# Loading the first pair's values before the third pair's queries and keys, and moving the third pair's roundings and first scores behind head 0's products

## The chip, the cores and the metric

One core of a Trainium2 chip runs the whole program. The metric is the device time of one execution in microseconds; a run is one execution, and the time given for a kernel is the median of its runs. The engines that the text names are TensorE (PE, with its weight loads PEld), VectorE (DVE), ScalarE (ACT), GpSimd (POOL) and SyncE (SP), which issues the DMAs.

## The reference

Attention with a decay, over 8 batches of 8 heads (576 positions, 64 columns each), and then a soft mixture of 8 small experts on the 4608 resulting rows. The change lies in the attention alone.

```python
scores = scale * np.matmul(q, k.transpose(0, 1, 3, 2))
log_f = np.log(np.clip(f, 0.0001, 1.0))
cum = np.cumsum(log_f, axis=-1)
decay = cum[:, :, :, None] - cum[:, :, None, :]
scores = np.where(causal, -1000000000.0, scores + decay)
scores = scores - np.max(scores, axis=-1, keepdims=True)
attn = np.exp(scores)
attn = attn / (np.sum(attn, axis=-1, keepdims=True) + 1e-09)
return np.matmul(attn, v).astype(np.float32)
...
logits = x @ phi
...
slot_input = d.T @ x
...
    h = np.maximum(slot_input[e] @ w1[e], 0.0)
    slot_out[e] = h @ w2[e]
...
return (c @ slot_out).astype(np.float32)
```

## The kernel before

The 64 heads are taken as 32 pairs (index g), two heads to a pair (h, or i = 2g + h over all heads). The program is written out in the order in which each engine runs it: an engine starts its instructions strictly in that order, each as soon as the counts that it waits for are reached.

A head goes through these steps. `load_qk` (L174) and `load_v` (L178) bring a pair's queries and keys (tile RAW, 576 KB) and its values (tile V, 325 KB) from memory. `round_k` and `round_q` (L183, L188, ACT) round keys and queries into WA and YA; `low_k` and `low_q` (L209, L214, POOL) compute what the rounding left off, into WB and YB, which also get a copy of the rounded part by DMA (`dup_k` L199, `dup_q` L203). `load_cum` (L194) brings the decay sums into two rows of WA. `s1` (L230, PE) makes a first set of scores in four pieces, each in a bank `s` of which there are three, and `tops` (L244, L246, DVE) takes their row maxima into MT. `mturn` (L256, PE) turns the maxima into a row, in columns 384 to 511 of the bank `pv` of that head; `mrows` copies that row out (L265, ACT, into the tile `mr`, of which there is one) and sends it by DMA into a row of YA (L268). `s2` (L283, L284, PE, banks `ring`) makes the exact transposed scores with the maxima taken off, `expo` (L290, ACT) their exponentials in PTS, `causal` (L298, L301, POOL) zeroes what lies above the diagonal. `s3` (L315, PE) multiplies them with the values into columns 0 to 324 of `pv`, one bank for each head of a pair; one entry of its list is one product of 64 queries with one block of keys, and the trace shows two matmul records for it. `norm` (L330 to L335, DVE) divides, and `px` (L342, PE) turns the result.

Heads 0 to 3 and the first pieces of head 4 are written out by hand, where the change lies; from g = 1 on a loop runs, one pass for a pair, in which the scores of heads 2g + 3 and 2g + 4 are made between those of heads 2g and 2g + 1. Its first instruction on PE is `s2` of head 2 (tile YA with 67 rows). `first(i, n)` is piece n of `s1` and its `tops`; `both(i, n)` is a piece of `s2` and its `expo`. The lists of `s3`, for head h:

```python
SIDES = [[x for n in zip(units(h, 0, range(4)), units(h, 1, range(4))) for x in n] for h in range(2)]
LAST = [units(h, h, (4,)) for h in range(2)]
```

`SIDES[h]` has 20 entries and `LAST[h]` 5. DMAs are all issued by SP, in program order, and spread over the core's DMA engines.

Of the kernel before, what the change touches and what calls it, by code (L numbers as in the profile page):

```python
# [47 lines left out]
def pt_col(c, i):  # L48
    at = {}
    for bank, cc, i0, w in SEGS:  # L50
        o = at.get(bank, 0)
        at[bank] = o + w
        if cc == c and i0 <= i < i0 + w:
            return SEG_O[bank] + o + i - i0
    raise ValueError


def queries(t, u):

    if t == 4:  # L60
        return 8
    return 2 * u + t if t < 2 else 4 + 2 * (1 - u) + t - 2


def units(h, u, ts):

    return [(h, t, u, c) for t in ts for c in range(queries(t, u) // 2 + 1)]


SIDES = [[x for n in zip(units(h, 0, range(4)), units(h, 1, range(4))) for x in n] for h in range(2)]  # L70
LAST = [units(h, h, (4,)) for h in range(2)]
# [3 lines left out]
def attn_softmoe(ctx: ExitStack, tc: tile.TileContext, qk, v, f, phi, w1, w2, cst, out):  # L75
# [78 lines left out]
    def pair(g):  # L154
        return 0 <= g < NG
# [15 lines left out]
    def load_qk(g):  # L171
        if pair(g) and ("r", g) not in st:
            st["r", g] = RAW[g % 3]
            nc.sync.dma_start(RAW[g % 3], qk[g])  # L174

    def load_v(g):
        if pair(g):
            nc.sync.dma_start(V[:, g % 2], v[g])  # L178

    def round_k(g, *hs):  # L180
        if pair(g):
            for h in hs or range(2):
                nc.scalar.copy(WA[g % 3][0:64, S * h : S * h + S], RAW[g % 3][64:128, h])  # L183

    def round_q(g, *hs):
        if pair(g):
            for h in hs or range(2):
                nc.scalar.copy(YA[g % 3][0:64, h, 64:640], RAW[g % 3][0:64, h])  # L188

    def load_cum(g):  # L190
        if pair(g):
            r0, r1 = CUM[g % 3]
            dst = WA[g % 3][r0 : r1 + 1 : r1 - r0, 0 : 2 * S].rearrange("c (h s) -> c h s", h=2)
            nc.sync.dma_start(dst.bitcast(F32), cumd[:, g].rearrange("h c s -> c h s"))  # L194

    def dup_k(g, h0=0, h1=2):
        if pair(g):
            s = slice(S * h0, S * h1)
            nc.sync.dma_start(WB[g % 2][64:128, s].bitcast(F32), WA[g % 3][0:64, s].bitcast(F32))  # L199
# [11 lines left out]
    def low_q(i):  # L211
        if head(i):
            g, h = divmod(i, 2)
            nc.gpsimd.tensor_tensor(YB[g % 2][64:128, h], RAW[g % 3][0:64, h], YA[g % 3][0:64, h, 64:640].bitcast(F32), op=ALU.subtract)  # L214
# [4 lines left out]
    def s1(i, *which):  # L219

        if not head(i):
            return
        g, h = divmod(i, 2)
        ya, wa, m = YA[g % 3], WA[g % 3][:, S * h : S * h + S], TOP[g % 3]
        for n in which:
            bank, o, blk, j0, w = TOPS[n]
            if o == 0:
                st["top", i % 2, bank] = scratch(False, f"s{i}_{bank}")
            t = st["top", i % 2, bank]
            nc.tensor.matmul(  # L230
                t[:, o : o + w], ya[0:m, h, 128 * blk : 128 * blk + 128], wa[0:m, j0 : j0 + w], start=True, stop=True
            )

    def tops(i, *which):
        if not head(i):
            return
        g, h = divmod(i, 2)
        for n in which:
            bank, o, blk, j0, w = TOPS[n]
            t = st["top", i % 2, bank]  # L240
            m0 = max(448 - (128 * blk + 64) + j0, 0)
            top = MT[g % 3][:, NBLK * h + blk : NBLK * h + blk + 1] if g else m2[h][:, blk, 1:2]
            if n == 2:
                nc.vector.tensor_reduce(top, t[:, o : o + w], axis=AX.X, op=ALU.max)  # L244
                continue
            nc.vector.tensor_tensor_reduce(  # L246
                out=t[:, o : o + w], in0=t[:, o : o + w], in1=mask[:, m0 : m0 + w], scale=1.0, scalar=top.bitcast(F32) if n == 3 else -3.0e38,
                op0=ALU.add, op1=ALU.max, accum_out=top,
            )

    def mturn(g, h0=0, h1=2):

        if not pair(g):
            return
        pm = pv[h0 and 1][:, 384:512]
        nc.tensor.transpose(pm[0 : NBLK * (h1 - h0), 0:128].bitcast(F32R), MT[g % 3][:, NBLK * h0 : NBLK * h1], turner)  # L256
        st["pm", g, h0] = pm

    def mrows(g, h0=0, h1=2):

        if not pair(g):
            return
        n = NBLK * (h1 - h0)
        mr = small.tile([2 * NBLK, P], F32R, name=f"mr{g}_{h0}", tag="mr", bufs=1)
        nc.scalar.copy(mr[0:n], st["pm", g, h0][0:n, 0:128])  # L265
        m = TOP[g % 3]
        dst = YA[g % 3][m : m + 1, h0:h1].rearrange("c h s -> c (h s)")
        nc.sync.dma_start(dst.bitcast(F32), mr[0:n].bitcast(F32))  # L268

    def s2(i, *which):  # L270
        if not head(i):
            return
        g, h = divmod(i, 2)
        ya, wa, yb, wb, m = YA[g % 3], WA[g % 3], YB[g % 2], WB[g % 2], TOP[g % 3] + 1
        for n in which:
            bank, c, i0, w = SEGS[n]
            t, at = (turn(), 0) if n < 4 else st["bank"]

            n = 128 if c < 4 else 64
            o = t[0:n, at : at + w]  # L280
            at += w
            j0 = S * h + 128 * c
            nc.tensor.matmul(o, wa[0:m, j0 : j0 + n], ya[0:m, h, 64 + i0 : 64 + i0 + w], start=True, stop=False)  # L283
            nc.tensor.matmul(o, wb[:, j0 : j0 + n], yb[:, h, i0 : i0 + w], start=False, stop=True)  # L284
            st["bank"] = t, at

    def expo(i, bank):
        if head(i):
            t, at = st["bank"]
            nc.scalar.activation(PT[i % 2][:, SEG_O[bank] : SEG_O[bank] + at], t[:, 0:at], AF.Exp, scale=0.125)  # L290

    def causal(i):

        if not head(i):
            return
        pt = PT[i % 2]
        d3 = pt[:, 0:960].rearrange("p (a b) -> p a b", b=320)[:, :, 0:128]
        nc.gpsimd.affine_select(d3, d3, pattern=[[0, 3], [1, 128]], compare_op=ALU.is_ge, fill=0.0, base=0, channel_multiplier=-1)  # L298
        for o, w in ((pt_col(3, 384), 128), (pt_col(4, 512), 64)):
            dd = pt[:, o : o + w]  # L300
            nc.gpsimd.affine_select(dd, dd, pattern=[[1, w]], compare_op=ALU.is_ge, fill=0.0, base=0, channel_multiplier=-1)  # L301
# [9 lines left out]
    def s3(g, todo):  # L311
        for h, t, u, c in todo:
            r = queries(t, u)
            at = pt_col(c, 64 * r)
            nc.tensor.matmul(  # L315
                pvv[h][64 * u : 64 * u + 64, t, :], PT[h][:, at : at + 64], V[:, g % 2, c, 65 * h : 65 * h + 65], start=(c == 0), stop=(c == r // 2)
            )
# [4 lines left out]
    def norm(i):  # L322
        if not head(i):
            return
        g, h = divmod(i, 2)
        b, p = divmod(g, NPAIR)
        x, o = xtile(b, p // 2), pvv[h]
        at = 128 * (p % 2) + 64 * h
        rl = small.tile([P, NBLK], F32, name=f"rl{i}", tag="rl")
        nc.vector.tensor_scalar_add(rl, o[:, :, 64], EPS)  # L330
        nc.vector.reciprocal(rl, rl)  # L331
        rl = rl.rearrange("p (t o) -> p t o", o=1)
        for ts in (slice(0, NBLK),) if i < NH - 1 else (slice(0, NBLK, 4), slice(1, 4)):
            to = x[:, ts, at : at + 64]
            nc.vector.tensor_tensor(to, o[:, ts, 0:64], rl[:, ts].broadcast_to(list(to.shape)), op=ALU.mult)  # L335
# [177 lines left out]
    def warm(n, a, w=192):  # L513

        for _ in range(n):
            nc.tensor.matmul(ring[0][:, 0:w], a[:, 0:128], a[:, 0:w], start=True, stop=True)  # L516
# [75 lines left out]
    round_k(1, 0)  # L592
    dup_k(1, 0, 1)
    load_cum(2)
    load_qk(2)
    load_v(0)

    def first_rows(h):
        part = ((0, 4), (4, 5))
# [12 lines left out]
    def first(i, n, busy=0):  # L612
        s1(i, *GROUPS[n])
        warm(busy, cs)
        tops(i, *GROUPS[n])

    def both(i, n):
        s2(i, *((0,), (1,), (2,), (3, 4, 5))[n])
        expo(i, n)
# [44 lines left out]
    both(1, 2)  # L664
    first(3, 2)
    first(3, 3)
    round_k(2, 0)
    round_q(2, 0)
    both(1, 3)
    causal(1)  # L670
    low_k(3)
    low_q(3)
    s3(0, SIDES[0][:20])
    first(4, 0)
    mturn(1, 1, 2)
    mrows(1, 1, 2)
    round_k(2, 1)
    round_q(2, 1)
    dup_q(2)
    dup_k(2)  # L680
    s3(0, SIDES[0][20:] + LAST[0])
    first(4, 1)
    first(4, 2)
    first(4, 3)
    norm(0)
    s3(0, LAST[1] + SIDES[1])
    load_cum(3)

    def fresh(stack, name, n):
# [469 lines left out]
```

## Time and profile before

| | |
|---|---|
| median of 3 runs | 385.81 us (385.1 to 386.08) |
| profiled execution | 385.02 us |
| its span | 383.3 us |
| PE, PEld busy | 95%, 86% |
| DVE, ACT, POOL busy | 74%, 70%, 67% |
| granted TensorE clock, mean | 0.986 |

The span is from the first to the last instruction that the profile records; the profiled execution's own time is 1.7 us more. Busy shares are averages over the whole span.

### The profile page before, as it was taken

What the parts mean: (1) busy time and instruction counts of PE and PEld (TensorE: products, weight loads), DVE (VectorE), ACT (ScalarE), POOL (GpSimd) and SP (SyncE); (2) the same over time, 40 slices, a digit from 0 to 9 for tenths busy, and PEclk for the clock granted to TensorE, in tenths of its full rate; (3) what the DMA queues carried; (4) which work ended last, traced back from release to release, by engine and by line L of the source; (5) the groups of instructions that cost most, each with busy time, mean ns of one, the idle gap of its engine ahead of it and who ended that gap; (6) DMA issues with size and microseconds to landing.
All of it is one profiled execution on the core that took longest, in us unless ns stands there. A gap on an engine that the chain in (4) does not pass through costs nothing.

```text
span 383.3 us, 15238 instructions
## 1 busy us (share of the span) xinstructions
PE 365.8 (95%) x5900; PEld 328.9 (86%) x5900; DVE 283.2 (74%) x1080; ACT 270.2 (70%) x656; POOL 258.6 (67%) x369
## 2 busy tenths in 40 slices
PE   8989999999999999999999999999999999999950
PEld 7888999999999999999999999999999986556650
DVE  7878887888878888888888888887888636443670
ACT  8859887878787878787878787878787654113550
POOL 4987887878797879787978797879787941010000
PEclk9999999999999999999999999999999999999995
DMA  6785778777868687768777777777777889999998
GB/s 190 197 207 163 227 232 264 203 224 210 252 180 249 195 251 197 231 197 245 208 216 218 225 215 220 213 221 216 218 214 213 264 290 377 414 405 393 310 326 291
DMA packets 37488, 93.72 MB, mean 245 GB/s; under 512 B 4412, under 2 KB 14380, under 8 KB 37416
## 3 DMA queue, kind: packets, MB, share of 16 engines
q1 hardware_dynamic: 37416, 92.75, 78.5%
q8 instruction: 46, 0.75, 0.8%
q14 instruction: 26, 0.21, 0.2%
HBM read 63.93 MB, written 9.73 MB: 192 GB/s over the span
## 4 chain that ended last, share of the span: by engine, by line
PE 91%; ACT 2%; DVE 1%; DMA 1%; POOL 1%; issue 0%; SPq 0%; DVEq 0%; POOLq 0%; ACTq 0%
PE pv L315 25%; PE ring L283 14%; PE s L230 13%; PE ring L284 13%; PE pv L342 4%; PE lg L389 3%; PE ring L516 2%; PE pv L1000 2%; PE ds L480 2%; PE ring L969 2%; PE pv L969 2%; PE ring L1000 2%; ACT PTS L290 1%; DMA V<-in_v 1%; PE ring L1084 1%; PE more L1084 1%
## 5 line engine op out<-in xcount | busy, mean ns | idle before, releaser
L290 ACT ACTIVATE PTS<-ring 128x320 f32<-128x320 f32 (+2 forms) x256 | 119.5, 500 | 38.1 <-PE ring L284 30.7
L283 PE MATMUL ring<-YA,WA 67*128 67x320 f32 (+9 forms) x384 | 118.8, 323 | 0.0
L246 DVE CUSTOM_DVE_ANT_0 s<-s,mask 128x320 f32<-128x320 f32 (+3 forms) x256 | 109.3, 445 | 8.1 <-PE s L230 2.4
L284 PE MATMUL ring<-YB,WB 128*128 128x320 f32 (+4 forms) x384 | 110.5, 296 | 0.0
L315 PE MATMUL pv<-V,PTS 128*64 128x65 f32 x3200 | 101.7, 223 | 1.1 <-POOL YB L214 1.0
L315 PEld LDWEIGHTS pv<-V,PTS 128*64 128x64 f32 x3200 | 96.9, 138 | 4.0 <-issue 1.2
L230 PE MATMUL s<-WA,YA 66*128 66x288 f32 (+9 forms) x384 | 97.9, 310 | 0.4 <-ACT PTS L290 0.3
L209 POOL TENSOR_TENSOR WB<-RAW,WB 64x576 fp32r<-64x576 f32 x64 | 90.9, 1420 | 10.5 <-DMA WB<-WA 5.4
L214 POOL TENSOR_TENSOR YB<-RAW,YA 64x576 fp32r<-64x576 f32 x64 | 89.8, 1421 | 2.5
L283 PEld LDWEIGHTS ring<-YA,WA 67*128 67x128 f32 (+3 forms) x384 | 68.9, 181 | 5.5 <-issue 2.1
L284 PEld LDWEIGHTS ring<-YB,WB 128*128 128x128 f32 (+1 forms) x384 | 69.9, 182 | 0.0
L230 PEld LDWEIGHTS s<-WA,YA 66*128 66x128 f32 (+1 forms) x384 | 63.0, 190 | 6.1 <-ACT YA L188 0.5
L246 DVE DVE_READ_ACCUMULATOR2_ANT MT<- 128x1 fp32r x310 | 43.9, 142 | 0.0
L301 POOL TENSOR_SCALAR_AFFINE_SELECT PTS<-PTS 128x128 f32<-128x128 f32 (+1 forms) x128 | 31.4, 266 | 17.1 <-ACT PTS L290 15.1
L183 ACT CAST WA<-RAW 64x576 fp32r<-64x576 f32 x63 | 39.5, 668 | 3.5 <-DMA RAW<-in_qk 2.7
L298 POOL TENSOR_SCALAR_AFFINE_SELECT PTS<-PTS 128x384 f32<-128x384 f32 x64 | 33.4, 522 | 12.7 <-ACT PTS L290 8.0
L188 ACT CAST YA<-RAW 64x576 fp32r<-64x576 f32 x62 | 39.4, 669 | 0.4
L246 DVE CUSTOM_DVE_ANT_0 s<-s,mask,MT 128x288 f32<-128x288 f32 x62 | 32.6, 526 | 9.0
L342 PE MATMUL pv<-cs,X 128*128 128x128 f32 x155 | 36.4, 272 | 0.0
L335 DVE TENSOR_TENSOR X<-pv,rl 128x320 f32<-128x320 f32 (+1 forms) x65 | 31.5, 486 | 2.4 <-DVE rl L331 0.3
L330 DVE TENSOR_SCALAR rl<-pv 128x5 f32<-128x5 f32 x64 | 10.5, 163 | 26.5 <-PE pv L315 21.1
L244 DVE TENSOR_REDUCE MT<-s 128x1 fp32r<-128x288 f32 x62 | 27.9, 451 | 0.7
(261 smaller groups left out, 383.5 us busy)
## 6 DMA issues: line engine op xcount, KB each, us to landing
w<-in_w SPq DMA_DIRECT2D x45, 512.0 KB
RAW<-in_qk SPq DMA_DIRECT2D x31, 576.0 KB
V<-in_v SPq DMA_DIRECT2D x32, 325.0 KB
YB<-YA SPq DMA_DIRECT2D x30, 288.0 KB
WB<-WA SPq DMA_DIRECT2D x30, 288.0 KB
p<-in_w SPq DMA_DIRECT2D x6, 512.0 KB
out<-RAW SPq DMA_DIRECT2D x12, 256.0 KB
out<-p SPq DMA_DIRECT2D x10, 256.0 KB
```

Source lines behind the costliest of these rows:

```text
L183: nc.scalar.copy(WA[g % 3][0:64, S * h : S * h + S], RAW[g % 3][64:128, h])
L188: nc.scalar.copy(YA[g % 3][0:64, h, 64:640], RAW[g % 3][0:64, h])
L209: nc.gpsimd.tensor_tensor(t[0:64], RAW[g % 3][64:128, h], t[64:128].bitcast(F32), op=ALU.subtract)
L214: nc.gpsimd.tensor_tensor(YB[g % 2][64:128, h], RAW[g % 3][0:64, h], YA[g % 3][0:64, h, 64:640].bitcast(F32), op=ALU.subtract)
L230: nc.tensor.matmul(t[:, o : o + w], ya[0:m, h, 128 * blk : 128 * blk + 128], wa[0:m, j0 : j0 + w], start=True, stop=True)
L246: nc.vector.tensor_tensor_reduce(out=t[:, o : o + w], in0=t[:, o : o + w], in1=mask[:, m0 : m0 + w], scale=1.0, scalar=top.bitcast(F32) if ...
L283: nc.tensor.matmul(o, wa[0:m, j0 : j0 + n], ya[0:m, h, 64 + i0 : 64 + i0 + w], start=True, stop=False)
L284: nc.tensor.matmul(o, wb[:, j0 : j0 + n], yb[:, h, i0 : i0 + w], start=False, stop=True)
L290: nc.scalar.activation(PT[i % 2][:, SEG_O[bank] : SEG_O[bank] + at], t[:, 0:at], AF.Exp, scale=0.125)
L298: nc.gpsimd.affine_select(d3, d3, pattern=[[0, 3], [1, 128]], compare_op=ALU.is_ge, fill=0.0, base=0, channel_multiplier=-1)
L315: nc.tensor.matmul(pvv[h][64 * u : 64 * u + 64, t, :], PT[h][:, at : at + 64], V[:, g % 2, c, 65 * h : 65 * h + 65], start=(c == 0), stop= ...
L342: nc.tensor.transpose(pm[:, 0:128], x[:, t, 128 * (p % 2) : 128 * (p % 2) + 128], ident)
```

## The change

In the part written by hand, four things move. Nothing is added or left out.

1. `load_v(0)` is issued before `load_qk(2)`.
2. The roundings of pair 2's first head (`round_k(2, 0)`, `round_q(2, 0)`) come after the last piece of head 1's scores and its exponential, not before.
3. All 25 products of head 0 come in one piece; `first(4, 0)`, which was between the 20th and the 21st, comes behind them.
4. `mturn(1, 1, 2)` and `mrows(1, 1, 2)` are now followed by eight products of head 1, and only then comes `first(4, 0)`, followed directly by the other three pieces of head 4's first scores.

```diff
     dup_k(1, 0, 1)
     load_cum(2)
+    load_v(0)
     load_qk(2)
-    load_v(0)
...
     first(3, 2)
     first(3, 3)
+    both(1, 3)
     round_k(2, 0)
     round_q(2, 0)
-    both(1, 3)
     causal(1)
     low_k(3)
     low_q(3)
-    s3(0, SIDES[0][:20])
-    first(4, 0)
+    s3(0, SIDES[0] + LAST[0])
     mturn(1, 1, 2)
     mrows(1, 1, 2)
+    s3(0, SIDES[1][:8])
+    first(4, 0)
     round_k(2, 1)
     round_q(2, 1)
     dup_q(2)
     dup_k(2)
-    s3(0, SIDES[0][20:] + LAST[0])
     first(4, 1)
     first(4, 2)
     first(4, 3)
     norm(0)
-    s3(0, LAST[1] + SIDES[1])
+    s3(0, LAST[1] + SIDES[1][8:])
     load_cum(3)
```

TensorE, from the first scores of head 4 on, before. In these rows pv_148 and pv_149 are the banks of head 0 and head 1, s_0 to s_3 the four pieces of head 4's first scores, WA_94 and YA_93 pair 2's rounded keys and queries, MT_109 the maxima of pair 1; a name in brackets is an engine, or a queue of DMAs, for whose count the row waits.

```order
L230 MATMUL s_0_395<-WA_94,YA_93 128x320 [waits DMAHW2_49,DMAHW7_49,DVE_49,Activation_49]
L230 MATMUL s_0_395<-WA_94,YA_93 128x192
L256 MATMUL pv_149<-turner,MT_109 5x128 [waits DVE_49]
L315 MATMUL pv_148<-V,PTS 64x65 x4
L315 MATMUL pv_148<-V,PTS 64x65 [waits Pool_49]
L230 MATMUL s_1_413<-WA_94,YA_93 128x288
L230 MATMUL s_2_416<-WA_94,YA_93 128x288
L230 MATMUL s_3_419<-WA_94,YA_93 128x448 [waits DVE_49]
L230 MATMUL s_3_419<-WA_94,YA_93 128x64
L315 MATMUL pv_149<-V,PTS 64x65 [waits Activation_49]
```

TensorE at the same place, with the change, from the last product of head 0 on.

```order
L315 MATMUL pv_148<-V,PTS 64x65 [waits Pool_49]
L256 MATMUL pv_149<-turner,MT_109 5x128 [waits DVE_49]
L315 MATMUL pv_149<-V,PTS 64x65 [waits Activation_49,Pool_49]
L315 MATMUL pv_149<-V,PTS 64x65 x7
L230 MATMUL s_0_412<-WA_94,YA_93 128x320 [waits DMAHW7_49,DMAHW2_49]
L230 MATMUL s_0_412<-WA_94,YA_93 128x192
L230 MATMUL s_1_421<-WA_94,YA_93 128x288
L230 MATMUL s_2_424<-WA_94,YA_93 128x288
L230 MATMUL s_3_427<-WA_94,YA_93 128x448 [waits DVE_49]
L230 MATMUL s_3_427<-WA_94,YA_93 128x64
L315 MATMUL pv_149<-V,PTS 64x65 x4
```

The first piece of head 4's scores has moved from before the turning to behind eight products of head 1, the wait for ACT has moved from that piece to the first of those products, and the four pieces now stand in a row.

ScalarE at that place; rows with a minus are those of before, mr_0 and mr_1 the copies of the maxima of pair 1's two heads (the second of them reads head 1's bank).

```order
 L265 CAST mr_0_340<-pv_148 5x128
 L290 ACTIVATE PTS<-ring_151 128x320
+L290 ACTIVATE PTS<-ring_152 128x512
 L183 CAST WA_94<-RAW_97 64x576
 L188 CAST YA_93<-RAW_97 64x576
-L290 ACTIVATE PTS<-ring_152 128x512
 L265 CAST mr_1_401<-pv_149 5x128
 L183 CAST WA_94<-RAW_97 64x576
```

The last exponential of head 1 has moved ahead of the two roundings of pair 2's first head; the copy of the second maxima stays behind both.

SyncE's DMAs at the place of the two loads.

```order
 L199 DMA WB_88<-WA_86 64x576
 L194 DMA WA_94<-cumd 2x2x576
-L174 DMA RAW_97<-in_qk 128x1152
-L178 DMA V<-in_v 128x650
+L178 DMA V<-in_v 128x650
+L174 DMA RAW_97<-in_qk 128x1152
 L203 DMA YB_87<-YA_85 64x576 x2
 L199 DMA WB_88<-WA_86 64x576
```

The two loads have changed places, and every other DMA stands where it stood.

## Rows read from the trace of the kernel before

**Rows 1.** The page: busy time, share of the span, instructions.

```profile
PE 365.8 (95%) x5900; PEld 328.9 (86%) x5900; DVE 283.2 (74%) x1080; ACT 270.2 (70%) x656; POOL 258.6 (67%) x369
```

**Rows 2.** Chain of waits, first 30 us: waiter, releaser, us, times, longest.

```profile
ACT mr L265 <- DMA YA<-mr: 2.1, 1, 2.1
```

**Rows 3.** Timeline, TensorE, 19.6 to 26.6 us: start, us, instructions [idle before].

```profile
19.60 0.22 PE L284 MATMUL ring<-YB,WB 128*64 128x64 f32 x1
20.83 1.39 PE L315 MATMUL pv<-V,PTS 128*64 128x65 f32 x40 [1.01 <-POOL YB L214]
22.15 0.50 PE L230 MATMUL s<-WA,YA 66*128 66x320 f32 x2
22.49 0.22 PE L256 MATMUL pv<-turner,MT 128*5 128x128 f32 x1
22.64 0.80 PE L315 MATMUL pv<-V,PTS 128*64 128x65 f32 x10
23.76 0.51 PE L230 MATMUL s<-WA,YA 66*128 66x448 f32 x2
24.20 1.96 PE L315 MATMUL pv<-V,PTS 128*64 128x65 f32 x50
26.09 0.47 PE L283 MATMUL ring<-YA,WA 67*128 67x448 f32 x1
```

**Rows 4.** Timeline, GpSimd: end of head 0's masking, and what follows.

```profile
18.78 0.49 POOL L301 TENSOR_SCALAR_AFFINE_SELECT PTS<-PTS 128x128 f32<-128x128 f32 x2
19.36 1.40 POOL L214 TENSOR_TENSOR YB<-RAW,YA 64x576 fp32r<-64x576 f32 x1
```

**Rows 5.** Timeline, ScalarE: rounding, last exponential of head 1, copy of the maxima.

```profile
19.09 0.67 ACT L183 CAST WA<-RAW 64x576 fp32r<-64x576 f32 x1
20.36 0.59 ACT L290 ACTIVATE PTS<-ring 128x512 f32<-128x512 f32 x1
23.06 0.26 ACT L265 CAST mr<-pv 5x128 fp32r<-5x128 f32 x1 [2.12 <-DMA YA<-mr]
```

**Rows 6.** Timeline, SyncE's issues: start and duration of the issue.

```profile
14.96 0.38 SPq L174 DMA_DIRECT2D RAW<-in_qk  x1
15.45 0.37 SPq L178 DMA_DIRECT2D V<-in_v  x1
18.44 0.76 SPq L268 DMA_DIRECT2D YA<-mr  x1
26.13 0.84 SPq L194 DMA_DIRECT2D WA<-cumd  x1
```

**Rows 7.** Busy time by windows: PE, PEld, DVE, ACT, POOL, clock, DMA share, GB/s.

```profile
16.00:18.00 2.00, 1.88 (x12) 1.49 (x11) 1.78 (x7) 1.34 (x3) 1.92 (x6) 1.00 0.93 286
24.00:26.00 2.00, 2.00 (x52) 1.86 (x51) 1.78 (x9) 0.68 (x2) 1.94 (x3) 1.00 0.11 23
...
53.00:61.70 8.70, 8.70 (x148) 8.37 (x146) 7.03 (x28) 7.22 (x18) 7.48 (x10) 1.00 0.87 250
```

**Rows 8.** Timeline, VectorE: maxima of head 4, then head 5's first and last.

```profile
22.69 0.50 DVE L246 CUSTOM_DVE_ANT_0 s<-s,mask 128x320 f32<-128x320 f32 x1 [2.09 <-PE s L230]
23.57 0.14 DVE L246 DVE_READ_ACCUMULATOR2_ANT MT<- 128x1 fp32r x1
23.81 0.46 DVE L244 TENSOR_REDUCE MT<-s 128x1 fp32r<-128x288 f32 x1
27.41 0.45 DVE L244 TENSOR_REDUCE MT<-s 128x1 fp32r<-128x288 f32 x1
30.26 0.14 DVE L246 DVE_READ_ACCUMULATOR2_ANT MT<- 128x1 fp32r x1
```

**Rows 9.** Timeline, TensorE weight loads around 30 us.

```profile
28.84 0.68 PEld L342 LDWEIGHTS pv<-cs,X 128*128 128x128 f32 x5
29.98 0.19 PEld L230 LDWEIGHTS s<-WA,YA 97*128 97x128 f32 x1 [0.47 <-ACT YA L188]
30.80 0.09 PEld L256 LDWEIGHTS pv<-turner,MT 128*10 128x10 f32 x1
```

## The prediction

> **What bounds the kernel now.** The page comes first: TensorE (PE) is busy for 365.8 us, 95% of the span [rows 1]. A stall of PE is time lost and a stall removed is time gained, unless a later stall swallows the difference. So the second view is the chain of waits over the first 30 us, where the change lies. It names one that comes to matter: ScalarE's copy of the maxima waited 2.1 us for the DMA that sends the earlier copy away [rows 2]. The third view is the timeline, engine by engine.
>
> PE ends head 1's scores at 19.60 + 0.22 = 19.82 and starts the first products at 20.83, after 1.01 us of standing [rows 3]. GpSimd's low part of pair 1's queries, named as releaser, ends just then, at 19.36 + 1.40 = 20.76 [rows 4]. But the products do not read it. What they need of GpSimd is head 0's masking, and that ended at 18.78 + 0.49 = 19.27 [rows 4]. The third thing they need is the values, whose load was issued at 15.45, behind the queries and keys of 14.96 [rows 6]. The DMA engines were 93% busy from 16 to 18 us, and down to 11% only from 24 on [rows 7]. I take it that the values landed near 20.8. The view prints no landing, so this is an inference; the other reading is a rival below.
>
> **The change, part by part.** The base is the profiled execution, 385.02 us (a span of 383.3 and 1.7 around it). The same difference is put on the median, 385.81. A measurement of this kernel can tell about 0.3% from no change, 1.16 us.
>
> *The two loads.* They keep their issue slots and their bytes, so what stands behind both should not move. The values come in front and queries and keys land where the values landed, near 20.8, 1.7 us later than the 19.09 at which ScalarE rounded them [rows 5]. PE can then start head 0's products at about 19.86 and not 20.83. Taken alone that is a gain of 1.0 us, its upper bound.
>
> *The roundings.* ScalarE first does head 1's last exponential (0.59 us, from about 19.85), then two roundings of 0.67 each [rows 5] from 20.8, done by 22.15. The copy behind them started at 23.06 [rows 5], so they fit with 0.9 us over. Cost nothing, as long as the load lands before 21.7.
>
> *Head 0's products.* In before 40 records took 22.15 - 20.83 = 1.32 us (33 ns each) and the last ten 0.80 [rows 3]. In one piece that is 2.1 us: from 19.86 they end at about 22.0, and the turning of the maxima, 0.15 us (22.49 to 22.64) [rows 3], ends at about 22.1.
>
> *Head 1's first eight products now stand right behind the turning.* This decides. In the order with the change the first of them waits for ScalarE, and head 4's first scores right behind, which need the rounded queries, have no wait for ScalarE any more. So the count waited for is not below that of the roundings, and the next thing in ScalarE's order is the copy of the maxima out of the same bank. The wait is for that copy. In before the same wait cost nothing, since head 1's first product came at 24.20 [rows 3]. The copy could not go before 23.06: there is one tile mr, and it waited for the DMA of the earlier maxima, issued at 18.44 [rows 2, 5, 6] and queued in the busy stretch [rows 7]. The bytes ahead of that DMA are the same after the change, so the copy still ends at 23.06 + 0.26 = 23.32, and PE restarts 0.05 later (as it did at 23.76 behind VectorE's end at 23.57 + 0.14 = 23.71 [rows 3, 8]), at 23.37. All that was gained at 19.8, and 0.3 more, is spent in a stall of 1.25 us. What is queued behind it is the rest of PE's program, and head 4's maxima on VectorE. No row of before shows this stall; its bounds are nothing (if the copy comes by 22.1) and 1.25, and I take the upper one, because the row of the copy is the nearest.
>
> The Trainium skill, PSUM — Partial Sum Buffer, section "PSUM bank collisions raise a hardware error", has a rule that speaks against this edit: guard PSUM by bank and quadrant, not by address, since another engine may not touch other columns of a bank in the same cycle. The copy reads columns 384 to 511, the products write columns 0 to 324; by address there would be no wait and the sum would come to nothing, by the rule it is the sum below. No trace row shows the rule itself; the order shows the wait.
>
> *Head 4's first scores in a row.* The eight products are 16 records of 33 ns, 0.53 us, so the first piece starts at 23.90, where before it started at 22.15 [rows 3]: 1.75 us later. There are three banks for the four pieces; the fourth piece waited in before until VectorE had finished the first, 23.76 - 22.15 = 1.61 us after the first piece's start [rows 3]. Then turning and products filled that time; now nothing does. Fourth piece at 25.51, products 24.20 - 23.76 = 0.44 later, at 25.95. There are 16 records fewer than the 50 of before, 26.09 - 24.20 - 0.53 = 1.36 us, so head 2's exact scores start at 27.31 and not 26.09: **1.22 us late**.
>
> *What swallows, what adds.* At 29.98 PE waited 0.47 us; ScalarE is named, but PE had loaded its last weights before at 28.84 + 0.68 = 29.52 [rows 9], and the scores there read the decay sums issued at 26.13 [rows 6]. That landing stays, since the copies before it hang on the copy of 23.06. Coming 1.22 late, PE gets there at 30.74 and no longer waits: 0.76 would be left. But VectorE is late too. It starts head 4 at 23.90 + 0.54 (22.69 - 22.15 [rows 3, 8]) = 24.44, has the first piece done 1.02 later (22.69 to 23.71), and begins the second at 25.46 where it began at 23.81 [rows 8]: 1.65 late. From there it is nearly without a gap to head 5's last maximum, which ended at 30.26 + 0.14 = 30.40 [rows 8] and now ends at 32.05. The turning of pair 2's maxima, at 30.80 in before [rows 9], waits for it: 32.10, **1.3 us late**. VectorE has slack behind that, PE has none; in a later pass, 53 to 61.7 us, PE is busy for all of 8.70 us [rows 7], so 1.3 stays to the end.
>
> **Sum.** 385.02 + 1.3 = 386.3 on the profiled execution; 385.81 + 1.3 = **387.1 us** on the median, 0.34% slower.
>
> **Rivals.**
> *The stall is short or absent* (not slower). If the earlier maxima's DMA lands sooner, because the DMA rings spread the reordered loads otherwise, the copy comes sooner. It decides quickly: landing 0.15 us sooner puts the sum under 1.16; by 21.75, instead of 23.0, PE does not stop at the turning. Then head 4 starts at 22.1 + 0.53 = 22.6, its fourth piece at 24.2, head 2 at 26.0; the wait at 29.98 remains and the time is 385.8. For it: nothing but that landings are not printed. Against it: equal bytes ahead.
> *Only part of it lasts* (same place, smaller): if VectorE closes gaps that I don't see, PE's own path leaves 0.8, 386.6.
> *The wait at 19.82 was for GpSimd after all.* Then products start at 20.83 again, the turning is done at about 23.1, the copy ends at 23.4: 0.1 more, 387.2. It does not change the verdict, since the start of the products is no longer on the path.
> *Queries and keys land late.* Past 21.7 the roundings push the copy in ScalarE's order, and with it the second head's roundings, their copies by DMA and the decay sums. Landing at 22.5 would add 0.8: 387.9.
> *Gain.* If the earlier maxima landed by 21.75, the copies and decay sums behind them would come earlier too and the wait at 29.98 would go: 0.47 off, 385.3. More than 1.16 has no mechanism here.
>
> The Trainium skill, DMA: Bandwidth & Descriptors, section "Queues, rings and completion order", says that descriptors on each DMA engine are consumed in ring order but completions are not in order of issue. By it the first rival could be true; the rows allow both, and its chance is below.
>
> **How the numbers follow.** Chances: the forecast, 1.0 to 1.6 us slower, 0.58; stall short or only part lasting, 0 to 1.0 slower, 0.25; queries and keys late, 1.6 to 2.5 slower, 0.11; gain, 0.06. The forecast lies close to the bound of 1.16, two thirds above it: slower 0.39 + 0.11 = 0.50. The same takes the other third, 0.19, and the short stall, 0.25: 0.44. Faster takes 0.06. The range leaves out the gain and half of the late landing: from 385.4 (no difference, less 0.4, about what the median of three runs that spread by 1 us can move) to 388.2. The forecast's own range is 386.8 to 387.4.
>
> **What would show it.** Right: PE starts products at about 19.9; it stands from about 22.1 to 23.4 between the turning and head 1's first product; the copy of the maxima starts at about 23.1, named as waiting for the DMA; a second stand of about 1.1 us before the fourth piece of head 4; no wait near 30 for the decay sums, but one of PE for VectorE before the turning at about 32. Wrong: a copy that starts before 22.5, products that start at 20.8, roundings that end past 23, or head 2's scores starting at 26.0 or earlier.

## The result, and the profile after

The changed kernel takes 387.74 us (median of 6 executions, 386.45 to 393.64) against 385.62 for the kernel before, 2.1 us more. The ratio is 1.0053, with a 95% interval from 1.0028 to 1.0079. Ratios, here and below, leave out executions over 1.5% above the fastest of their kernel (here the 393.64; below, three of the eleven of the changed kernel in its second run, and one execution of 698 to 1948 us of each of three kernels), and medians leave out none. The profile below is of the 393.64 execution, and it shows why it is so long.

The page of the changed kernel, first busy time and then the granted clock in 40 slices, in tenths:

```profile
span 391.9 us, 15238 instructions
PE 371.8 (95%) x5900; PEld 334.5 (85%) x5900; DVE 283.8 (72%) x1080; ACT 271.1 (69%) x656; POOL 258.4 (66%) x369
PEclk9985899999999999999999999999999999999995
```

PE is busy 6.0 us longer than in before [rows 1] with the same instructions. The fourth slice, from 29.4 to 39.2 us, has half the clock, and the slices beside it 0.8. The timeline of TensorE after the change, which answers to [rows 3]:

```profile
19.67 1.96 PE L315 MATMUL pv<-V,PTS 128*64 128x65 f32 x50
21.56 0.22 PE L256 MATMUL pv<-turner,MT 128*5 128x128 f32 x1
23.91 0.69 PE L315 MATMUL pv<-V,PTS 128*64 128x65 f32 x16 [2.13 <-ACT mr L265]
24.53 0.79 PE L230 MATMUL s<-WA,YA 66*128 66x320 f32 x4
26.14 0.80 PE L230 MATMUL s<-WA,YA 66*128 66x448 f32 x2 [0.82 <-DVE MT L246]
26.87 2.65 PE L315 MATMUL pv<-V,PTS 128*64 128x65 f32 x34
29.44 0.74 PE L283 MATMUL ring<-YA,WA 67*128 67x448 f32 x1
```

Head 0's products start at 19.67 and not at 20.83, and run without a stop. Behind the turning PE stands for 2.13 us until ScalarE's copy of the maxima is done; behind three of head 4's pieces it stands again, 0.82 us, for VectorE. Then the matmuls take longer: head 2's first matmul (the last row) takes 0.74 us, where it took 0.47 in before [rows 3]. ScalarE in the same stretch, which answers to [rows 5]:

```profile
20.89 0.67 ACT L183 CAST WA<-RAW 64x576 fp32r<-64x576 f32 x1 [0.52 <-DMA RAW<-in_qk]
23.51 0.25 ACT L265 CAST mr<-pv 5x128 fp32r<-5x128 f32 x1 [1.26 <-DMA YA<-mr]
```

Queries and keys landed at 20.9, as far as the rounding that waits for them shows it, and the copy waited for the DMA of the earlier maxima until 23.5. Busy time by windows after the change (clock in the third column from the right):

```profile
22.00:24.00 2.00, 0.09 (x3) 0.12 (x5) 0.00 (x0) 0.71 (x3) 0.63 (x1) 1.00 0.99 341
26.00:28.00 2.00, 1.86 (x16) 1.64 (x17) 1.82 (x10) 0.00 (x0) 2.00 (x3) 0.50 0.76 145
28.00:40.00 12.00, 12.00 (x73) 11.31 (x72) 7.00 (x26) 5.98 (x15) 3.90 (x6) 0.50 0.39 105
40.00:42.00 2.00, 2.00 (x42) 2.00 (x42) 0.59 (x4) 1.94 (x4) 1.37 (x3) 0.50 0.01 5
44.00:46.00 2.00, 2.00 (x22) 1.89 (x16) 1.59 (x6) 1.49 (x4) 1.39 (x2) 1.00 1.05 203
```

One of these windows in before:

```profile
28.00:40.00 12.00, 11.74 (x165) 10.84 (x163) 9.98 (x40) 11.45 (x27) 9.30 (x15) 1.00 0.67 184
```

PE worked 0.09 us of the two from 22 to 24. From 26 on the granted clock is 0.50, that is 1.2 GHz of 2.4, and it is back at 1.00 from 44 on; in before it was 1.00 all that time. The two levels are those of the Trainium skill, TensorE: Matmul & The Clock Gate, "Part 1: The HAM clock gate", by which the array's clock is 2.4 GHz when PE has been busy and 1.2 when it has idled, with nothing between. The trace agrees on the levels, but not on the return: PE was busy for all of the 14 us from 28 to 42, and the clock stayed at 0.50.

### The profile page after: what moved, and what is told of

Its sections match the earlier page's. It is cut to its first block, busy times and chain, and to the rows that moved or that the text cites. A ratio compares the mean times of both kernels' runs of the same rounds, so it can differ in the third digit from the quotient of the medians.

```text
span 391.9 us, 15238 instructions
## 1 busy us (share of the span) xinstructions
PE 371.8 (95%) x5900; PEld 334.5 (85%) x5900; DVE 283.8 (72%) x1080; ACT 271.1 (69%) x656; POOL 258.4 (66%) x369
## 4 chain that ended last, share of the span: by engine, by line
PE 89%; DMA 3%; POOL 2%; DVE 1%; ACT 1%; issue 1%; DVEq 0%; POOLq 0%; ACTq 0%
PE pv L315 25%; PE ring L283 15%; PE ring L284 13%; PE s L230 13%; PE pv L342 4%; PE lg L389 3%; PE pv L1000 2%; PE ds L480 2%; PE ring L969 2%; PE pv L969 2%; PE ring L1000 2%; DMA YA<-mr 1%; PE ring L1084 1%; POOL YB L214 1%; DMA PTS<-in_f 1%
## 5 line engine op out<-in xcount | busy, mean ns | idle before, releaser
L283 PE MATMUL ring<-YA,WA 67*128 67x320 f32 (+9 forms) x384 | 120.8, 328 | 0.0
L284 PE MATMUL ring<-YB,WB 128*128 128x320 f32 (+4 forms) x384 | 112.3, 300 | 0.0
L315 PE MATMUL pv<-V,PTS 128*64 128x65 f32 x3200 | 104.2, 225 | 2.2 <-ACT mr L265 2.1
L315 PEld LDWEIGHTS pv<-V,PTS 128*64 128x64 f32 x3200 | 99.3, 140 | 5.1 <-issue 3.7
L230 PE MATMUL s<-WA,YA 66*128 66x288 f32 (+9 forms) x384 | 99.6, 315 | 1.9 <-DVE WA L565 0.9
L283 PEld LDWEIGHTS ring<-YA,WA 67*128 67x128 f32 (+3 forms) x384 | 70.5, 185 | 5.4 <-issue 2.1
L284 PEld LDWEIGHTS ring<-YB,WB 128*128 128x128 f32 (+1 forms) x384 | 71.5, 186 | 0.0
L230 PEld LDWEIGHTS s<-WA,YA 66*128 66x128 f32 (+1 forms) x384 | 64.6, 195 | 7.7 <-DVE MT L246 1.3
L330 DVE TENSOR_SCALAR rl<-pv 128x5 f32<-128x5 f32 x64 | 10.5, 164 | 28.9 <-PE pv L315 23.5
```

The costliest lines, as they stand in the source:

```text
L230: nc.tensor.matmul(t[:, o : o + w], ya[0:m, h, 128 * blk : 128 * blk + 128], wa[0:m, j0 : j0 + w], start=True, stop=True)
L315: nc.tensor.matmul(pvv[h][64 * u : 64 * u + 64, t, :], PT[h][:, at : at + 64], V[:, g % 2, c, 65 * h : 65 * h + 65], start=(c == 0), stop= ...
```

## The experiments

All ratios are against the kernel before on the same chip. "Low clock" counts the executions with a mean granted clock of 0.985 or less, without the three longest. The runs are from three chips, on which before itself had 4 of 34, 14 of 35 and 5 of 15: the first is that of the changed kernel, the first stall filled, the other bank and the swap, the second that of both stalls filled, the two own places and the first piece ahead, the third that of the last row and of the two single executions below.

| kernel | median us | ratio, 95% interval | low clock |
|---|---|---|---|
| changed, again | 388.57 | 1.0051 [1.0021, 1.0081] | 8 of 11 |
| dummy matmuls in the first stall | 387.24 | 1.0044 [1.0026, 1.0061] | 3 of 12 |
| dummy matmuls in both stalls | 386.64 | 1.0014 [0.9998, 1.0031] | 0 of 11 |
| turning into the other bank | 386.08 | 1.0010 [0.9993, 1.0028] | 4 of 12 |
| own place for the first copy | 386.80 | 1.0012 [0.9985, 1.0040] | 6 of 12 |
| before, loads swapped | 386.57 | 1.0034 [1.0010, 1.0057] | 8 of 12 |
| before, own place for the copy | 386.09 | 0.9983 [0.9955, 1.0012] | 3 of 11 |
| before, first piece ahead | 384.83 | 0.9964 [0.9948, 0.9981] | 0 of 11 |
| the same, another chip | 384.86 | 0.9970 [0.9956, 0.9984] | 2 of 10 |

**The changed kernel again.** No edit.

> The changed kernel once more, to see more of its executions. Theory: the stall between the turning and head 1's first product costs about 1 us (386.5 with the clock held, as in the fastest execution so far, 386.45 at a mean granted clock of 0.988), and the rest of the measured difference is TensorE's clock, which falls from 2.4 to 1.2 GHz behind the two stalls (from 25.6 us on in the profiled execution) and comes back after a stretch whose length differs between executions: times and mean clocks go together, 386.4 to 389, and every execution whose mean clock is under 0.987 has a stretch at half clock that begins right behind the stalls. Rival: the clock falls by chance anywhere in the program, and the stall alone gives 1.3 us or more also at a held clock.

Its eleven executions fall into three groups by the mean clock: three at 0.989 took 385.7 to 386.1 us, four at 0.984 to 0.985 took 387.8 to 389.0, four at 0.968 to 0.969 took 391.4 to 393.1. The arithmetic fits roughly: 0.005 of the mean clock is 2 x 0.005 x 387 = 3.9 us at half clock, and PE-bound work then takes about half of that longer, 1.9 us (measured 2.5); 0.0205 is 16 us at half clock and 8 us longer (measured 6.6). The three took less than the theory's 386.5 at a held clock, and only 0.4 us more than before did at a held clock (medians 385.85 and 385.46 us, over the executions with a mean clock of 0.986 or more); none of them was traced. The timeline of the profiled one, of 388.98 us:

```profile
24.30 0.69 PE L315 MATMUL pv<-V,PTS 128*64 128x65 f32 x16 [2.29 <-ACT mr L265]
22.64 0.67 ACT L183 CAST WA<-RAW 64x576 fp32r<-64x576 f32 x1 [2.05 <-DMA RAW<-in_qk]
23.90 0.25 ACT L265 CAST mr<-pv 5x128 fp32r<-5x128 f32 x1
```

Busy time by windows in the same execution:

```profile
26.00:28.00 2.00, 1.48 (x18) 1.35 (x20) 1.82 (x8) 0.00 (x0) 2.00 (x2) 0.80 0.54 105
28.00:30.00 2.00, 2.00 (x25) 1.84 (x23) 1.51 (x10) 0.00 (x0) 1.73 (x2) 0.50 0.99 199
30.00:32.00 2.00, 2.00 (x15) 1.96 (x13) 1.56 (x5) 1.44 (x4) 0.00 (x0) 0.84 0.56 166
```

Here queries and keys landed at 22.6, and the copy stood behind the two roundings. The stall is much the same, 2.29 us; the clock was half for about 3.4 us only, from 27.2 to 30.6 (worked out from the means of the first and the last window, 0.80 and 0.84).

**Two more executions of it, each with a trace.**

> The changed kernel, one look. Two of its traces show the clock falling behind the stalls; three of its eleven timed executions held 0.989 and took 385.7 to 386.1. Theory: where the clock holds, the earlier maxima landed sooner (22.2 to 22.7 instead of 23.5), TensorE stood 0.7 to 1.2 us between the turning and head 1's products, and products of the first pass start 0.3 to 0.7 us later than in before (32.30). Rival: an equally long stall (2.1 us) with the clock held, and the delay swallowed later.

> The changed kernel, a second look, with the same two theories as the first: a held clock goes with a short stall, or else a stall of 2.1 us with a held clock and the delay swallowed later. A look with the clock fallen should show the stall above 1.8 us and the fall within 5 us behind it.

They took 389.48 (clock 0.981) and 392.84 us (0.969). TensorE's product behind the turning, in the first and in the second:

```profile
23.82 0.69 PE L315 MATMUL pv<-V,PTS 128*64 128x65 f32 x16 [1.89 <-ACT mr L265]
```

```profile
24.74 0.69 PE L315 MATMUL pv<-V,PTS 128*64 128x65 f32 x16 [2.97 <-ACT mr L265]
```

Windows of the second:

```profile
36.00:38.00 2.00, 2.00 (x11) 2.00 (x10) 0.53 (x2) 1.65 (x6) 1.56 (x2) 0.50 0.00 0
40.00:42.00 2.00, 2.00 (x68) 1.96 (x67) 1.06 (x6) 1.71 (x3) 1.00 (x3) 1.00 0.02 7
```

In all four traces of the changed kernel the stall was 1.9 to 3.0 us and the clock fell within 5 us behind it. None was caught with the clock held, so whether the executions with a held clock had a short stall, as the theory of both runs has it, stays open.

**Dummy matmuls in the first stall, and in both.**

```diff
     mturn(1, 1, 2)
     mrows(1, 1, 2)
+    warm(6, cs)
     s3(0, SIDES[1][:8])
```

The second kernel has `warm(5, cs)` there and also:

```diff
     first(4, 2)
+    warm(2, cs)
     first(4, 3)
```

> Six dummy matmuls (192 columns each, about 0.32 us apiece by the start of the trace, 1.95 us together) stand between the turning of the maxima and head 1's first product, where TensorE stood for 2.1 us. They save no waiting: head 1 still waits for the copy. Theory (the clock falls because TensorE stands): the clock holds in all executions, 386.3 to 386.8, faster than the changed kernel by about 1 us, with less spread. Rival (the clock has nothing to do with the standing): the same as the changed kernel, 387.7 with the same spread. Second rival (the shorter stall of 1 us before the fourth piece of head 4 is what drops it): same as the changed kernel too, with the clock falling right after that stall.

> The changed kernel with five dummy matmuls in the first stall (1.8 us) and two in the second, before the fourth piece of head 4 (0.7 us). Theory (the clock falls because TensorE stands, and either stall can do it): no execution with a mean clock under 0.987, 386.2 to 386.8, a narrower spread than with the first stall alone filled, where 5 of 12 executions were at 0.985 to 0.986 and up to 389.6. Rival (the fall is by chance): again some executions at 0.985 or below and a spread of 3 us.

The timeline of the first, with ScalarE's copy among TensorE's rows:

```profile
21.64 2.16 PE L516 MATMUL ring<-cs 128*128 128x192 f32 x12
22.94 0.26 ACT L265 CAST mr<-pv 5x128 fp32r<-5x128 f32 x1 [0.36 <-DMA YA<-mr]
23.73 0.69 PE L315 MATMUL pv<-V,PTS 128*64 128x65 f32 x16
27.82 0.47 PE L283 MATMUL ring<-YA,WA 67*128 67x448 f32 x1
32.47 0.09 PEld L256 LDWEIGHTS pv<-turner,MT 128*10 128x10 f32 x1 [0.31 <-ACT XTS L375]
```

A window of the same execution:

```profile
26.00:28.00 2.00, 2.00 (x37) 1.80 (x38) 1.78 (x9) 0.00 (x0) 2.00 (x3) 1.00 1.06 204
```

The dummies saved no waiting; the copy ended at 23.20 and they held PE half a microsecond too long. Yet the clock stayed at 1.00 in this trace, and head 2's first matmul took 0.47 us, as in [rows 3]. It came at 27.82, 1.73 later than in before, and the span is 384.8 us, 1.5 over before. With one stall filled, 3 of 12 executions were still low, against 8 of 11 for the changed kernel on the same chip; so the stand in the first stall is what lowers the clock in a good part of its executions. The theory's 386.3 to 386.8 in all executions was missed all the same: five of the twelve lie in it, and some of the others took up to 387.7 us at a mean clock of 0.987 to 0.990, which no trace explains. With both stalls filled none was low, and the median fell from 388.57 to 386.64 (the two on different chips; by the ratios from 1.0051 to 1.0014), with eleven executions within 1.3 us. That the second stall of 0.82 us lowers the clock too is what these counts suggest and not shown: in the trace above it did not, the three low executions were not traced, and the only trace with both stalls filled is of the execution of 697.52 us, in which the matmuls took about one and a half times as long. The row at 32.47 is the turning of pair 2's maxima, read further down.

**The turning into the other bank.**

```diff
-        pm = pv[h0 and 1][:, 384:512]
+        pm = pv[0][:, 384:512]
```

> The changed kernel with the second turning's output put into head 0's bank, so that head 1's products no longer share a bank with the copy; all else is as changed. Theory (the wait for the copy is the loss): products follow the turning at once, head 4's first piece starts at about 22.3, behind the roundings, head 2's exact scores at about 25.9, and the time is that of before within 0.3%: 385.3 to 386.0. Rival (the loss comes from queries and keys that land late, or from VectorE's wait with the four pieces in a row): 386.5 or more.

Its timeline, with ScalarE's copy among TensorE's rows:

```profile
21.65 0.22 PE L256 MATMUL pv<-turner,MT 128*5 128x128 f32 x1
21.80 0.69 PE L315 MATMUL pv<-V,PTS 128*64 128x65 f32 x16
22.45 0.79 PE L230 MATMUL s<-WA,YA 66*128 66x320 f32 x4
22.88 0.26 ACT L265 CAST mr<-pv 5x128 fp32r<-5x128 f32 x1 [0.47 <-DMA YA<-mr]
24.07 0.50 PE L230 MATMUL s<-WA,YA 66*128 66x448 f32 x2 [0.82 <-DVE MT L246]
25.92 0.47 PE L283 MATMUL ring<-YA,WA 67*128 67x448 f32 x1
29.82 0.37 PE L230 MATMUL s<-WA,YA 97*128 97x288 f32 x1 [0.18 <-DMA WA<-cumd]
```

The row of before that answers to the last of these:

```profile
30.01 0.37 PE L230 MATMUL s<-WA,YA 97*128 97x288 f32 x1 [0.26 <-ACT PTS L290]
```

With the copy in a bank that nobody else writes then, head 1's products follow the turning at once, 1.1 us ahead of the copy, and the ratio is 1.0010, not to be told from none (the median, 386.08, is just above the theory's range). The program's waits go by the rule in the Trainium skill, PSUM — Partial Sum Buffer, section "PSUM bank collisions raise a hardware error", cited with the prediction: in the changed kernel the products wait for a copy out of other columns of their bank, and here, with another bank, they do not. No run lets products and copy into one bank at once, so what the chip would do then is not shown. Head 2's scores start at 25.92, 0.17 before [rows 3]; the wait near 30 us, which stands here as one for the decay sums, does not take that back, for the scores behind it start at 29.82 and not at 30.01.

**An own place for the first copy of maxima**, in the changed kernel and in before.

```diff
-        mr = small.tile([2 * NBLK, P], F32R, name=f"mr{g}_{h0}", tag="mr", bufs=1)
+        if (g, h0) == (1, 0):
+            mr = EX[0 : 2 * NBLK, 0:128].bitcast(F32R)
+        else:
+            mr = small.tile([2 * NBLK, P], F32R, name=f"mr{g}_{h0}", tag="mr", bufs=1)
```

> The changed kernel with a place of its own for the first copy of maxima (a part of a tile that is free so early), so that the second copy no longer waits for the DMA of the first; head 1's products still wait for the second copy. Theory: the copy follows the roundings at about 22.3 where these end then, TensorE stands 0.7 us instead of 2.1 between the turning and head 1's products, the clock holds in nearly all executions, and the time is 385.7 to 386.2; in executions in which queries and keys land late (after 22) the stall stays. Rival (the copy's own wait is not what holds the products): products and time as in the changed kernel, 387.7 or more.

Its timeline in the changed kernel (line numbers are 3 higher here from `mrows` on):

```profile
22.06 0.25 ACT L268 CAST mr<-pv 5x128 fp32r<-5x128 f32 x1
22.46 0.69 PE L318 MATMUL pv<-V,PTS 128*64 128x65 f32 x16 [0.67 <-ACT mr L268]
26.54 0.47 PE L286 MATMUL ring<-YA,WA 67*128 67x448 f32 x1
```

The copy ran at 22.06, right behind the roundings, and the stall shrank from 2.13 to 0.67 us. Six of twelve executions kept the clock (mean 0.987 or more) and took 385.5 to 386.5. The theory had the clock held in nearly all executions and 385.7 to 386.2; six were low, and the median is 386.80. So the copy's wait for the earlier DMA is part of what makes the stall long: it came last in three of the four traces of the changed kernel (1.26, 0.89 and 1.08 us of waiting), while in the fourth the late roundings did.

> The kernel before with a place of its own for the first copy of maxima. Theory (the wait of 0.47 us near 30 us hangs on the copy that waited until 23.06): the second copy starts near 22.8, behind its turning, the decay sums are issued 0.25 us sooner, and the wait near 30 us shrinks by as much: 385.2 to 385.5, 0.2 us or no visible difference. Rival (the wait near 30 is for ScalarE's rounding, as the view names it): it stays at 0.47.

In before the ratio with it is 0.9983 [0.9955, 1.0012]: no difference that can be told. In its trace the copy waited for the turning, 2.37 us, no longer for the DMA; but the values came later still than in [rows 3], so the gain could not show:

```profile
21.44 1.39 PE L318 MATMUL pv<-V,PTS 128*64 128x65 f32 x40 [1.55 <-DMA V<-in_v]
23.36 0.26 ACT L268 CAST mr<-pv 5x128 fp32r<-5x128 f32 x1 [2.37 <-PE pv L256]
```

The first line also names the values as what PE waits for there. Its stand of 1.55 us was not followed by a fall: the granted clock is 1.00 in every window from 20 to 46 us.

**Before with the two loads swapped.**

```diff
-    load_qk(2)
     load_v(0)
+    load_qk(2)
```

> The kernel before with the two loads swapped and nothing else. Theory: head 0's products start at 19.9 and not at 20.8, but head 4's first piece then waits for the late roundings until about 22.3, and what is left is taken by the wait for the decay sums near 30 us: the time of before within 0.3%, 385.3 to 386.0. Rival (the earlier products last to the end): 1.0 us faster, 384.6.

Neither theory gave this: 0.34% slower, and 8 of 12 executions with a low clock. Its timeline:

```profile
19.64 1.39 PE L315 MATMUL pv<-V,PTS 128*64 128x65 f32 x40
22.89 0.61 PE L230 MATMUL s<-WA,YA 66*128 66x320 f32 x2 [1.86 <-ACT YA L188]
21.49 0.67 ACT L183 CAST WA<-RAW 64x576 fp32r<-64x576 f32 x1 [2.52 <-DMA RAW<-in_qk]
```

And a window behind it:

```profile
24.00:26.00 2.00, 2.00 (x13) 1.67 (x11) 0.98 (x5) 1.31 (x2) 1.94 (x2) 0.50 0.09 25
```

The products do start at 19.64. But 1.0 us of standing before them has become 1.86 us behind them, on the queries and keys, and the clock falls. The swap alone moves the stall and makes it longer. The four executions with a mean clock of 0.987 or more took 384.9 to 386.0 us, which is the time of before, as the theory had it; the loss is in the other eight.

**Before with head 4's first piece and the turning ahead of head 0's products.** It has the own place for the first copy as well.

```diff
     low_k(3)
     low_q(3)
-    s3(0, SIDES[0][:20])
     first(4, 0)
     mturn(1, 1, 2)
...
     dup_q(2)
     dup_k(2)
-    s3(0, SIDES[0][20:] + LAST[0])
+    s3(0, SIDES[0] + LAST[0])
     first(4, 1)
     first(4, 2)
```

> The kernel before, loads in its order, with the separate place for the first copy, and with head 4's first piece and the second turning moved ahead of head 0's products, into the wait for the values, and the second head's roundings right behind the copy. Theory: head 4's first piece starts at 20.5 instead of 22.15, products at about 20.95, the second copy at about 21.0 instead of 23.06, head 2's exact scores at about 25.4 instead of 26.09, no wait near 30 us: 1.0 to 1.3 us faster than before, 384.2 to 384.5. Rival (VectorE or the decay sums give it back): 385.2 to 385.6.

> The same kernel as the one with head 4's first piece and the second turning ahead of head 0's products, once more, on a chip of its own draw, for a trace at its usual time. Theory: 384.4 to 385.0 and 0.2 to 0.4% under before; in the trace head 4's first piece starts near 20.5, head 0's products near 20.9, the second copy near 21.0, head 2's exact scores near 25.4, no wait for the decay sums near 29, and TensorE's clock stays at 2.4 GHz. Rival (the first comparison was helped by a chip on which before fell to the lower clock more often): no more than 0.1% under before.

It is 0.36% and 0.30% under before on two chips, with intervals that leave out 1, where the changed kernel's ratios are above 1. The rival does not explain it: among executions with a mean clock of 0.986 or more it took 384.82 against 385.81 us on the first chip and 384.61 against 385.94 on the second (medians). The loads stay in the order of before, and the wait for the values holds work. The timeline is of the slowest of the second chip's ten executions (386.64 us):

```profile
20.78 0.50 PE L230 MATMUL s<-WA,YA 66*128 66x320 f32 x2 [0.69 <-ACT YA L188]
21.69 3.24 PE L318 MATMUL pv<-V,PTS 128*64 128x65 f32 x50 [0.35 <-DMA V<-in_v]
21.39 0.26 ACT L268 CAST mr<-pv 5x128 fp32r<-5x128 f32 x1 [0.16 <-PE pv L256]
```

One of its windows:

```profile
22.00:24.00 2.00, 2.00 (x41) 2.00 (x38) 0.34 (x2) 1.01 (x2) 0.70 (x2) 0.50 0.99 347
```

Head 4's first piece starts at 20.78 and the copy at 21.39, against 22.15 and 23.06 in [rows 3, 5]. In this execution the clock fell even behind the short stands of 0.69 and 0.35 us, and head 2's scores came at 27.68 and not at the 25.4 of the expectation; one other of these ten had a mean clock of 0.985 or less, and none of the eleven on the first chip. No trace shows an execution with the full gain. Whether the piece, the turning or the separate place brings most of the gain was not taken apart; the place by itself showed none that can be told (0.9983, above).

## Why the prediction was right, point by point

*The mechanism was right.* Head 0's products started at 19.67 (19.86 forecast), the turning was done at 21.78 (22.1; the sum had 2.1 us for the fifty product records, which took 1.96), PE then stood until ScalarE's copy was done, and stood again before the fourth piece of head 4. The fourth piece came 1.61 us behind the first piece, as worked out from [rows 3]. The bank experiment shows that the wait for the copy is the cause: without the shared bank PE does not stand there, and the ratio is 1.0010 and not 1.0051 (its interval, up to 1.0028, leaves room for a smaller loss from something else).

*The values were what PE waited for in before.* After the change GpSimd's low part still ends where it did, at 19.28 + 1.42 = 20.70, and the products start 1.2 us earlier, before it ends:

```profile
19.28 1.42 POOL L214 TENSOR_TENSOR YB<-RAW,YA 64x576 fp32r<-64x576 f32 x1
```

The rival in which GpSimd was the releaser is out.

*The landing of the earlier maxima was mis-sized.* The prediction kept it at 23.0, with equal bytes ahead. By the start of the copy it was 23.5, 23.4 and 24.3 in three traces of the changed kernel; in a fourth the copy had to wait for the roundings until 23.9. That is the rival of late queries and keys, and it does occur: they landed between 20.9 and 22.6. With the turning done earlier, the stall was 1.9 to 3.0 us and not 1.25. What decides which transfer lands late in an execution was not tried.

*The step that was missing is the clock.* The sum had 1.3 us for delayed work and nothing for what standing does to PE afterwards. As it stands the changed order costs 0.51 to 0.53%, and 1.8 to 2.1% in the executions over 390 us that the ratios leave out; with both stalls filled the ratio is 1.0014, which cannot be told from 1. That ratio flatters the order, because before had a low clock in 14 of its 35 executions on that chip: among executions with a mean clock of 0.986 or more it is 386.58 against 385.81 us, 0.8 us. The forecast of 387.1 was too low because of the clock, 387.74 and then 388.57 measured. The clock appears in neither the terms nor the rivals, and the upper end, 388.2, held the first median but not the second. That the first median came within 0.6 us of the forecast is therefore luck in part: five of its six executions had a mean clock of 0.985 or less.

*The size of the delayed work is not settled.* In the trace with dummies PE restarted at 23.73 and reached head 2's scores 4.09 us later; the prediction had 3.94 (23.37 to 27.31). The end came 1.5 us after that of before, and half a microsecond of it is the dummies' own. So 1.0 us is left for the 1.3 forecast, from one execution of each kernel. Other executions at a held clock give less: 0.8 us with both stalls filled, and 0.4 us in the three of the changed kernel. Whether these three had the short stall of the first rival, or a long one that was swallowed later, is open.

*What holds the turning of pair 2* was named wrongly. It waited, 0.31 us, but the trace with dummies names ScalarE's copy of head 0's transposes out of the same bank, ended at 32.41, beside VectorE's last maximum at 32.35. The number came out near: 32.10 forecast, 32.47 with the half microsecond of the dummies in it.

*The wait near 30 us for the decay sums* vanished in the changed kernel and stands in the bank experiment, where the view names that DMA for the matmul (0.18 us), though ScalarE's rounding once more for its weight load (0.39 us).

## What to carry to other kernels

A stall has two prices: the time that the engine stands, and on TensorE what comes after, because stands of 1.9 to 3.0 us were followed by 3 to 17 us at half clock in four of four traces of the changed kernel. Before moving a transfer forward, ask whose landing it pushes back, and put work that needs neither transfer into the wait that is already there. In this program a copy out of a bank holds the products that go into that bank, so a row that is turned in a shared bank should be copied out before its neighbours are due.

## What the runs showed of the hardware that was not expected

In eleven executions of one program the times fall into three groups, 386, 388 and 392 us, that go with TensorE's mean clock; single executions lie between (389.05 us at 0.980, 389.48 at 0.981). Each of the four traces has one fall behind the first stall, and its length, worked out from the windows, does not follow that of the stall: 6.8 us behind a stall of 1.89 us, 17.0 behind 2.13, 3.4 behind 2.29 and 13.7 behind 2.97. In one trace the clock fell behind stands of only 0.69 and 0.35 us, while in others stands of 0.82, 1.01 and 1.55 us were followed by no fall. Before, which stands for 1.0 us in its trace, had a mean clock of 0.985 or less in 4 of 34, 14 of 35 and 5 of 15 executions on three chips; none of these was traced. And with the same DMAs ahead of it the small one that holds the copy landed between 22.9 and 24.3 us in five traces with the changed order of the loads, at 23.4 and 24.3 in two executions of one program on one chip.
